# A recurrent attention kernel: its next-memory product moved into column tiles, its first transposes moved from DMA to TensorE, and its order searched again

## Chip, cores, metric

One core of one Trainium2 chip. The metric is device time of one launch in microseconds (us), the median of several executions. A ratio is the mean time of one kernel's runs over the mean of the other's runs of the same rounds, so it isn't quite the ratio of the medians quoted beside it. Where I turn a ratio into microseconds I multiply by 1869, the time before.

## The reference, cut to what matters

```python
def _A_ref(x, mem0, Wq, Wk, Wv, Wo, seg_len):      # S 2048, Dm 512, H 32, Dh 128, M 8, seg 32
    mem = mem0
    for s in range(S // seg_len):                    # 64 segments, one after the other
        h = concatenate([mem, xs])                   # 8 memory rows + 32 tokens
        q, k, v = (einsum('btd,dhe->bhte', h, W) for W in (Wq, Wk, Wv))
        p = softmax(where(mask, q @ k.T * scale, -1e9))
        o = einsum('bhte,hed->btd', p @ v, Wo)
        mem = o[:, :M, :]                            # the memory of the next segment
        outs.append(o[:, M:, :])
# x = x + A(layernorm(x)); x = x + B(layernorm(x)); and both once more
# B: linear attention over all 2048 tokens with 32 heads of 16
```

Layer A is a recurrence: segment s+1 can't be projected before segment s has gone through attention, the output projection and back into `mem`. There are 2 x 64 such steps. B of the first layer must be complete before the second A starts.

## The kernel before

The kernel is a program that writes a program. Every operation is a node with a cost; a list scheduler runs a clock of its own, gives each node an engine and a place, and the places are steered by priorities (`OFFSET`, one number for each node of a step). TensorE's products come in two kinds: the whole 128x128 array ("full"), and column tiles ("col"), where four products of 32 output columns each share the array. The scheduler charges 0.1 us for a change between them.

```python
PE_SWITCH = 0.1
...
            nd.start = max(tn, rtime(nd))
            if e == "pe":
                if nd.mode != self.pe_mode:
                    nd.start += PE_SWITCH
                self.pe_mode = nd.mode
```

A projection is four groups of four products in tiles. Its image is copied out of PSUM and turned, either by a DMA transpose issued from SP or by 16 TensorE transposes and one more copy:

```python
        def turned(W, key, blk, bkeys, b, dst, dkey, urgent, dma):
            tl = project(W, key, blk, bkeys, b, urgent)
            k = img_no[0] % NI if urgent else NI          # the left block has one buffer for all its images
            ...
            nd = evac(img[:, k, :], lambda: tl.f32()[:, :], 512, ...)
            if dma:
                add("sp", lambda e: e.dma_start_transpose(dst..., img[:, k, :]), 1.25, ..., lat=TURN)
                return nd
            ...  # 16 x pe.transpose(..., tile_position=(0, 32 * j)), then evac
```

The four tiles of the output projection each hold a part of the sum over heads (and a half of the columns), so the next memory is the sum over row groups of `outW`, done by a product with a 0/1 matrix. The same `outW` also goes through selection products into the residual (whole array, f32r):

```python
        def next_mem(s, w):
            at(s, "next")
            for h in range(2):
                def mm(pe, h=h):
                    return pe.matmul(tl.f32()[:, 16 * h:16 * h + 16], outW[:, w, 128 * h:128 * h + 128], selm_sb[:, :],
                                     start=True, stop=True)
                add("pe", mm, 0.13, reads=[("outW", w, h), "selm"], tiles=[tl], urgent=True)
            evac(hT[:, G1 % 2, g1, :, 0:8]..., urgent=True)   # into the next segment's input
```

A "left block" collects the last 8 tokens of each of 4 segments, is projected once for 4 steps, and serves as filler for TensorE while the recurrence waits.

The softmax here doesn't subtract the row's maximum and nothing guards it: scores larger than these inputs give would overflow.

## Time and profile before

| | before |
|---|---|
| median, us | 1869.8 (1865.6 to 1870.0, 3 runs) |
| profiled run, span | 1867.5 |
| TensorE / ScalarE / VectorE busy | 94% / 62% / 57% |
| first next-memory product of layer 1 | 60.7 us |
| 62 steps of layer 1 | 831.3 us, 13.41 a step |
| turn to layer 2 (63rd to 64th product) | 67.5 us |
| 62 steps of layer 2 | 841.5 us, 13.57 a step |
| tail | 66.5 us |

The rows of the view by stretches up to the first next-memory product and from there to the last of layer 1 (columns: length, busy time of PE, PEld, DVE, ACT, POOL with counts, granted clock, DMA share, GB/s):

```profile
0.00:60.70 60.70, 29.96 (x478) 14.13 (x478) 12.73 (x35) 16.98 (x44) 13.94 (x61) 0.84 0.93 310
60.70:891.90 831.20, 813.34 (x20871) 562.67 (x20912) 487.35 (x1536) 533.04 (x1393) 25.48 (x47) 1.00 0.21 41
```

Three lines follow. The first is the summary of the page's chain of waits, the shares of the span by engine. The other two are the product that changes, from the view of its source line: weight loads (PEld) and products (PE), count, and the duration in ns as min/median/max.

```profile
PE 85%; DMA 10%; ACT 2%; DVE 2%; issue 1%; SPq 0%; ACTq 0%; DVEq 0%
...
L975 PEld LDWEIGHTS pb<-selm_sb,outW_sb x252: 185/186/337, 60.6 to 1801.3; 128*128 128x128 f32 x126
L975 PE MATMUL pb<-selm_sb,outW_sb x252: 256/277/362, 60.7 to 1801.3; 128*128 128x16 f32 x126
```

There are 252 of them, two for each of 126 steps. A duration is the time from start to modelled end; products overlap, so what one costs the queue is how far it moves the end on, and I use that below ("the advance").

### The profile page before, as it was taken

To read this page: it belongs to the slowest core of one execution; us is meant where nothing else is said; L and a number is where in the kernel's file an instruction comes from. 1 tells how busy PE (TensorE), PEld (TensorE's weight loads), DVE (VectorE), ACT (ScalarE), POOL (GpSimd) and SP (SyncE) were. 2 spreads that over 40 slices of the span, in tenths; PEclk is the share of its full clock that TensorE was granted. 3 is DMA by queue.
4 is the path that set the end of the run, shared out by engine and by line. 5 is a ranking of instruction groups with operands and counts; after the bars stand their busy time and mean duration, and the time that the engine had idled before them with its cause. 6 is when DMAs were issued, how large, how long until landed. Compare 5 with 4: busy or idle time off the path is not lost.

```text
span 1867.5 us, 95161 instructions
## 1 busy us (share of the span) xinstructions
PE 1762.9 (94%) x43796; PEld 1201.8 (64%) x43905; DVE 1065.5 (57%) x3267; ACT 1160.3 (62%) x3015; POOL 74.5 (4%) x172
## 2 busy tenths in 40 slices
PE   4899999999999999999799999999999999999996
PEld 1566767666666667676456666766667666676662
DVE  1455555656565565655445556556555665565555
ACT  2466666666666666666456666666666666666655
POOL 2000000000000000000000000000000000000000
PEclk8999999999999999999899999999999999999999
DMA  9512121221222121211021222122122221212213
GB/s 336 126 35 42 35 43 37 43 40 37 43 37 43 35 46 37 45 38 40 21 42 35 42 38 48 40 37 45 37 44 42 45 43 38 45 38 54 45 34 124
DMA packets 228256, 96.86 MB, mean 52 GB/s; under 512 B 211624, under 2 KB 222000, under 8 KB 226320
## 3 DMA queue, kind: packets, MB, share of 16 engines
q1 hardware_dynamic: 220656, 62.58, 18.1%
q0 software_dynamic: 5616, 15.60, 2.7%
q10 hardware_dynamic: 1584, 12.58, 1.7%
q8 instruction: 343, 5.62, 1.3%
q14 instruction: 57, 0.47, 0.1%
HBM read 29.89 MB, written 10.49 MB: 22 GB/s over the span
## 4 chain that ended last, share of the span: by engine, by line
PE 85%; DMA 10%; ACT 2%; DVE 2%; issue 1%; SPq 0%; ACTq 0%; DVEq 0%
PE pb L753 39%; PE pb L952 15%; DMA arena_sb<-arena_sb 8%; PE pb L928 4%; PE pb L837 3%; PE pb L775 3%; PE pb L993 3%; PE pb L1088 2%; PE pb L975 2%; PE pb L854 2%; PE pb L892 2%; PE pb L1124 1%; PE pb L868 1%; PE pb L1190 1%; PE pb L867 1%
## 5 line engine op out<-in xcount | busy, mean ns | idle before, releaser
L591 ACT ACTIVATE arena_sb<-pb 128x512 bf16<-128x512 f32 (+6 forms) x1309 | 682.0, 530 | 341.5 <-PE pb L753 272.5
L753 PE MATMUL pb<-Wk_sb,arena_sb 128*32 128x512 bf16 x5120 | 347.7, 383 | 5.5 <-DMA Wk_sb<-in_A_Wk_dram 5.5
L753 PE MATMUL pb<-Wv_sb,arena_sb 128*32 128x512 bf16 x5120 | 352.2, 381 | 0.0
L753 PE MATMUL pb<-Wq_sb,arena_sb 128*32 128x512 bf16 x5120 | 342.2, 383 | 5.4 <-DVE arena_sb L592 4.8
L952 PE MATMUL pb<-Wo_sb,arena_sb 128*32 128x256 bf16 x10368 | 312.3, 275 | 4.9 <-DMA Wo_sb<-in_A_Wo_dram 2.9
L592 DVE CAST arena_sb<-pb 128x128 bf16<-128x128 f32 (+3 forms) x452 | 179.9, 398 | 221.3 <-PE pb L975 110.0
L952 PEld LDWEIGHTS pb<-Wo_sb,arena_sb 128*32 128x32 bf16 x10368 | 274.2, 97 | 20.7 <-DMA Wo_sb<-in_A_Wo_dram 3.4
L913 DVE TENSOR_TENSOR arena_sb<-arena_sb 32x256 bf16<-32x256 bf16 x512 | 212.1, 414 | 50.9 <-ACT arena_sb L909 38.8
L592 DVE COPY arena_sb<-pb 128x512 bf16<-128x512 bf16 (+2 forms) x325 | 121.2, 380 | 191.6 <-PE pb L775 183.9
L753 PEld LDWEIGHTS pb<-Wk_sb,arena_sb 128*32 128x32 bf16 x5120 | 136.9, 97 | 133.6 <-DMA Wk_sb<-in_A_Wk_dram 5.6
L753 PEld LDWEIGHTS pb<-Wq_sb,arena_sb 128*32 128x32 bf16 x5120 | 124.2, 96 | 111.3 <-DVE arena_sb L592 10.6
L753 PEld LDWEIGHTS pb<-Wv_sb,arena_sb 128*32 128x32 bf16 x5120 | 132.5, 97 | 98.1 <-issue 2.8
L591 ACT ACTIVATE outW_sb<-pb 128x128 fp32r<-128x128 f32 x228 | 63.2, 277 | 200.0 <-PE pb L952 198.0
L775 PEld LDWEIGHTS pb<-id_sb,arena_sb 128*32 128x32 bf16 x4096 | 76.4, 96 | 95.0 <-ACT arena_sb L591 47.5
L775 PE MATMUL pb<-id_sb,arena_sb 128*32 128x128 bf16 x4096 | 103.1, 220 | 24.1 <-ACT arena_sb L591 20.2
L928 PE MATMUL pb<-arena_sb 128*128 128x128 bf16 x1024 | 118.7, 217 | 5.5 <-DVE arena_sb L915 5.5
L592 DVE CAST outW_sb<-pb 128x128 fp32r<-128x128 f32 x96 | 28.0, 292 | 161.6 <-ACT outW_sb L591 161.6
L915 DVE TENSOR_TENSOR arena_sb<-arena_sb 32x64 bf16<-32x64 bf16 x512 | 110.8, 216 | 15.7
L844 ACT ACTIVATE arena_sb<-pb 128x256 bf16<-128x256 f32 x252 | 92.1, 383 | 41.1 <-PE pb L837 33.1
L929 PE MATMUL pb<-arena_sb 128*128 128x32 bf16 x1024 | 109.7, 178 | 0.0
L928 PEld LDWEIGHTS pb<-arena_sb 128*128 128x128 bf16 x1024 | 87.8, 96 | 7.2 <-DVE arena_sb L915 5.9
L837 PE MATMUL pb<-arena_sb 128*128 128x32 bf16 x2016 | 89.3, 177 | 2.8 <-DMA arena_sb<-arena_sb 2.5
(109 smaller groups left out, 2270.2 us busy)
## 6 DMA issues: line engine op xcount, KB each, us to landing
arena_sb<-arena_sb SPq DMA_TRANSPOSE x384, 2.5
Wq_sb<-in_A_Wq_dram ACTq DMA_DIRECT2D x1, 4096.0 KB, 13.5
Wk_sb<-in_A_Wk_dram ACTq DMA_DIRECT2D x1, 4096.0 KB, 23.7
Wv_sb<-in_A_Wv_dram ACTq DMA_DIRECT2D x1, 4096.0 KB, 34.4
Wo_sb<-in_A_Wo_dram SPq DMA_DIRECT2D x4, 1024.0 KB, 7.5
xs_scratch<-x_sb POOLq DMA_DIRECT2D x32, 128.0 KB, 2.0
pq_scratch<-arena_sb POOLq DMA_DIRECT2D x32, 128.0 KB, 2.5
x_sb<-xs_scratch POOLq DMA_DIRECT2D x16, 128.0 KB, 2.3
```

What stands on the lines that cost most here:

```text
L591: return e.activation(o() if callable(o) else o, i() if callable(i) else i, ACTF.Copy)
L592: return e.tensor_copy(o() if callable(o) else o, i() if callable(i) else i)
L753: r = pe.matmul(tl.f32()[32 * j:32 * j + 32, 0:512], blk[:, c, :], W[:, c, o:o + 512], start=(c == 0), stop=(c == 3), tile_position=(0, 32 ...
L775: r = pe.transpose(tt.bf16()[32 * j:32 * j + 32, 128 * i:128 * i + 128], img[:, k, o:o + 32], id_sb[:, :], tile_position=(0, 32 * j))
L837: r = pe.matmul(tl.f32()[:, o:o + 32], kk[:, hh, :, :].rearrange("p j x -> p (j x)"), qT[:, r2, hh, :, 0:8], start=True, stop=True)
L844: add("act", lambda a: a.activation(Pm[:, k, :, :].rearrange("p a q -> p (a q)"), tl.f32()[:, 0:256], ACTF.Exp, scale=SCALE), c_act(256), ...
L913: add("dve", lambda v, q=q, j=j: v.tensor_tensor(Pbx[q, :, j, 0:32], Px[q, :, :], Rx[q, :, :], ALU.mult), c_dve(256) + 0.075, reads=["Px", ...
L915: add("dve", lambda v, q=q, j=j: v.tensor_tensor(Pbx[q, :, j, 32:40], PLL[q, g2, :, gl], Rx[q, :, 0:8], ALU.mult), c_dve(64) + 0.075, read ...
L928: pe.matmul(o, vimg[:, r2, e], Pbx[:, hh, :, 0:32], start=True, stop=False)
L929: return pe.matmul(o[:, :, 0:8], vleft[:, g2, e], Pbx[:, hh, :, 32:40], start=False, stop=True)
L952: r = pe.matmul(tl.f32()[32 * j:32 * j + 32, 0:256], oT[:, 4 * hh + n, :], Wo_sb[:, 8 * n + hh, 256 * d:256 * d + 256], start=(hh == 0 and ...
L993: r = pe.matmul(tl.f32()[:, 256 * d:256 * d + 256], sel(d), outW[:, u, :], start=first and d == 0, stop=last, skip_group_check=True)
```

## The change

The intent: (1) make the next-memory product cheaper and of the same kind as the products around it, so that the array needn't change between whole and tiles; (2) in the first step and the first left block of each layer transpose on TensorE, since nothing else fills it there; (3) search the priorities again.

```diff
-MODE_SLACK = 13.03
-LOOK = 0.073
+MODE_SLACK = 13.61
+LOOK = 0.082
 ... (every list of OFFSET has new numbers; the first step has lists of its own)
-            P.at(base + s, name + ("F" if s < 0 else "L" if ...))
+            P.at(base + s, name + ("F" if s <= 0 else "L" if ...))
 ...  left_block
-                turned(Wq_sb, "Wq", blk, bk, b, qTl[:, r2, hs, :, :], ("qTl", r2, b), False, True)
+                turned(Wq_sb, "Wq", blk, bk, b, qTl[:, r2, hs, :, :], ("qTl", r2, b), False, step > 0)
 ... (the same for Wk)
 ...  next_mem
                 def mm(pe, h=h):
-                    return pe.matmul(tl.f32()[:, 16 * h:16 * h + 16], outW[:, w, 128 * h:128 * h + 128], selm_sb[:, :],
-                                     start=True, stop=True)
-                add("pe", mm, 0.13, reads=[("outW", w, h), "selm"], tiles=[tl], urgent=True)
+                    for j in range(4):
+                        o = 128 * h + 32 * j
+                        r = pe.matmul(tl.f32()[32 * j:32 * j + 32, 16 * h:16 * h + 16], outW[:, w, o:o + 32].bitcast(F32),
+                                      selm_sb[:, :].bitcast(F32), start=True, stop=True, tile_position=(0, 32 * j))
+                    return r
+                add("pe", mm, 0.075, reads=[("outW", w, h), "selm"], tiles=[tl], urgent=True, mode="col")
 ...  the step
-                turned(Wq_sb, "Wq", blk, bk, b, qT[:, r2, hs, :, :], ("qT", r2, b), True, QDMA[b])
+                turned(Wq_sb, "Wq", blk, bk, b, qT[:, r2, hs, :, :], ("qT", r2, b), True, QDMA[b] and s > 0)
 ... (the same for Wk)
```

## The prediction

> **What bounds the kernel now.** I read the page's busy shares first, then the stretches of its span, then TensorE's groups, and last the two starts in the timeline.
>
> ```profile
> PE 1762.9 (94%) x43796; PEld 1201.8 (64%) x43905; DVE 1065.5 (57%) x3267; ACT 1160.3 (62%) x3015; POOL 74.5 (4%) x172
> ```
>
> TensorE is busy 94% of the span, the next engine 62%. An average hides stages, so I asked for five stretches: until the first output projection, the steps of layer 1 (first to last next-memory product), the turn to layer 2, the steps of layer 2, the tail. The columns are the length, then busy time of each engine, then granted clock.
>
> ```profile
> 0.00:57.20 57.20, 26.46 (x407) 11.36 (x411) 12.73 (x35) 15.83 (x41) 13.94 (x61) 0.85 0.95 317
> 57.20:891.90 834.70, 816.84 (x20942) 565.45 (x20986) 487.35 (x1536) 534.19 (x1396) 25.48 (x47) 1.00 0.21 42
> 891.90:959.50 67.60, 50.53 (x907) 28.61 (x909) 29.27 (x77) 27.95 (x67) 2.92 (x6) 0.85 0.15 31
> 959.50:1801.00 841.50, 824.46 (x20986) 572.07 (x21043) 500.19 (x1546) 549.22 (x1450) 30.95 (x57) 1.00 0.21 42
> 1801.00:1867.50 66.50, 44.56 (x563) 24.32 (x566) 35.96 (x75) 33.09 (x64) 1.22 (x3) 0.92 0.32 96
> ```
>
> In both runs of steps TensorE is busy 98% at full clock: there only work taken from TensorE counts. Both have 62 full steps: 831.3/62 = 13.4 us and 841.5/62 = 13.6 us a step. At the start it is busy 46% of 57 us, and there something else sets the end. The chain of waits on the page gives TensorE 85% and DMA 10%; the DMA part of a step (about 4 us of a transpose) is covered by other TensorE work, so I don't count it as time to win.
>
> **The next-memory product** as one step has it in the timeline (start, length):
>
> ```profile
> 705.96 0.27 PE L892 MATMUL pb<-arena_sb 128*32 128x32 bf16 x16
> 706.16 0.39 PE L975 MATMUL pb<-selm_sb,outW_sb 128*128 128x16 f32 x2
> 706.40 0.48 PE L993 MATMUL pb<-outW_sb,selx_sb 128*128 128x256 f32 x2
> 706.84 0.50 PE L993 MATMUL pb<-outW_sb,sell_sb 128*128 128x256 f32 x2
> 707.19 0.28 PE L904 MATMUL pb<-arena_sb,bo_sb 128*128 128x256 bf16 x1
> 707.31 0.19 PE L905 MATMUL pb<-arena_sb,bo_sb 128*128 128x64 bf16 x1
> 707.43 0.40 PE L753 MATMUL pb<-Wq_sb,arena_sb 128*32 128x512 bf16 x4
> ```
>
> L975 is the product that changes. Lines with 128*32 work in column tiles, those with 128*128 in the whole array; the sequence goes tiles, whole array, tiles.
>
> **The first step of the kernel.** What the SP queue issued, and what TensorE then waited for:
>
> ```profile
> 16.95 2.61 SPq L766 DMA_TRANSPOSE arena_sb<-arena_sb  x2
> 24.96 0.39 SPq L629 DMA_DIRECT2D Wo_sb<-in_A_Wo_dram  x1
> 34.28 7.78 SPq L766 DMA_TRANSPOSE arena_sb<-arena_sb  x3
> 42.11 0.58 SPq L629 DMA_DIRECT2D Wo_sb<-in_A_Wo_dram  x1
> 45.30 1.19 SPq L766 DMA_TRANSPOSE arena_sb<-arena_sb  x1
> 46.53 2.83 SPq L629 DMA_DIRECT2D Wo_sb<-in_A_Wo_dram  x2
> 57.16 0.51 PE L952 MATMUL pb<-Wo_sb,arena_sb 128*32 128x256 bf16 x12 [2.94 <-DMA Wo_sb<-in_A_Wo_dram]
> ```
>
> The first output projection waits for the last quarter of Wo. The quarters landed at 39.6, 49.0, 53.5 and 57.1 us (semaphore events). The second may leave once Wv is there (36.2 us), but stood behind transposes on SP until 42.1.
>
> **What the Trainium skill says.** (1) "TensorEngine Tiling (Array Packing)", Key Properties: changing the tiling mode drains TensorE. The trace agrees: in order of start there are 276 changes each way (2.2 a step). A projection's first four products end 0.22 us after work in tiles and 0.32 after whole-array work; the first L975 ends 0.207 us after tiled work, the second 0.112 after the first. So a change costs about 0.1 us. (2) "FP8 and Floating Point Precision", TensorE Precision Notes: true FP32 takes 4 passes. No plain f32 product is in this trace. (3) "TensorE: Matmul & The Clock Gate", Back-to-back issue gap: starts are never under about 25 ns apart. The trace agrees for whole-array products of 32 columns (25 ns apart); 16 in tiles advance 6.3 ns each, 25 ns for four.
>
> **The change part by part.**
> Next memory: an L975 pair costs 0.112 x 2 = 0.22 us, and its changes 0.1 each way. The selection sums rows, so the new form puts 32 columns of the head-half output into each of four column tiles: 8 products of 16 columns. Four passes for each group of four tiles at the 25 ns floor are 0.10 us, so 0.20 a step; if the passes stream as 64 columns, 0.03 a group and 0.05 a step. Both are estimates; I take 0.15, so the product alone saves 0.07. The larger gain is that the neighbours are also in tiles (output projection before, q projection after), so the pair of changes, 0.2 us, can go, but only where the 0.5 us between this product and the next q is filled with tiled work. With residual and sums (L993, L904) there, as above, the changes stay. Left-block projections are not in every step, so I count three tenths of the steps: 0.06. Together 0.13 x 126 = 16 us, all on the bound engine.
> Start of layer 1: no transposes stand before Wo on SP. The second quarter can leave at 36.2. At the 344 GB/s this queue moved in the stretch when it had only Wo, 1 MB takes 3.05 us: after the first at 39.6, the others land at 42.7, 45.7, 48.8. V, due 36.2, and the 26 us of TensorE work before L952 fit, since TensorE had 31 us idle there. 57.1 - 48.8 = 8 us off the path.
> Start of layer 2: from 930.7 to 959.5 step 0 takes 28.8 us against a later 13.4, with TensorE busy 24.8 of it at clock 0.86. The left block's four transposes share one image buffer and each holds it for some 4 us (median landing 2.5 us after issue). On TensorE a set of 16 takes 0.23 us of throughput and a copy of 0.42. At most 4.0 idle and 24.8 x 0.14 = 3.5 us of low clock can be won; 6 x 0.23 = 1.4 us is added. I take 3 net.
> Order: work at its own pace (each product at the median spacing of its kind) sums to 1617 us, the changes to 552 x 0.1 = 55; ends and turn leave about 105 idle. Some 90 us, 0.7 a step, remain as small stalls. The search of before could not remove them; I give the new one 4.
> Sum: 16 + 8 + 3 + 4 = 31, so 1869.8 - 31 = 1839 us.
>
> **The rivals.** (a) *The changes stay and f32 is slow.* If a pass is dearer than the floor, the product saves nothing, and if full-array fill sits before and after it, two more changes come: 0.2 x 126 = 25 us lost. For it: steps without left work have only L904, L905 and L993 to fill. Against: the order is chosen to avoid it. Only starts would gain: 1855 to 1865. (b) *Wo doesn't bound the first step.* If V at half clock (1.9 us for 16 products at 41 us) bounds it, the first step gains 4 instead of 8: 1843. (c) *Every pair of changes goes.* Then 0.27 x 126 = 34 us and the starts: 1820. Against it: the residual must run in the whole array somewhere, though it could join the memory attention. (d) *A transpose by DMA becomes the wait.* When TensorE takes less time a step, its 4 us cover may fail. TensorE's slack of 2% says the cover is good now; a loss would be some tenths a step, giving 1850.
>
> **Range and chances.** The product is worth 5 to 30 us, the first start 4 to 10, the second 0 to 6, the order -5 to 12; they're independent, so roughly +-18 on the sum: 1821 to 1857. Over 2% faster means below 1832.4, a third of a range's width below my centre: 0.28. Slower than 1907 needs a broken order: 0.01.
>
> **What would show it.** L975 in tiles: the time from the end of the work before it to its last product under 0.2 us against 0.32; mode changes below 2.2 a step, toward 1.8; the first output projection near 49 us; first L975 of layer 2 some 3 us sooner after the layer's start; a step of 13.2 to 13.3 us against 13.4 and 13.6; no other engine over 70%. I am wrong if f32 products in tiles have long starts (over 0.1 us a group), if Wo still lands after 53 us, or if the step gains over 0.25 us.

## The result, and the profile after

The changed kernel takes 1854.2 us (median of 4, 1851.7 to 1855.9) against 1869.3 (4 runs): ratio 0.9922, 95% interval 0.9905 to 0.994. That is 14.6 us less, where I had forecast 31. The span of the profiled run is 1850.0 us.

The view by stretches of the changed kernel, cut at the same events as in the table above (length, busy time of PE, PEld, DVE, ACT, POOL, then granted clock, DMA share, GB/s):

```profile
0.00:54.60 54.60, 31.69 (x604) 16.65 (x604) 15.35 (x43) 18.09 (x47) 13.97 (x61) 0.91 0.90 324
54.60:883.60 829.00, 810.60 (x21712) 551.82 (x21752) 469.05 (x1478) 557.76 (x1447) 25.22 (x46) 1.00 0.21 42
883.60:941.70 58.10, 45.92 (x970) 27.23 (x973) 28.16 (x75) 26.31 (x65) 3.26 (x6) 0.88 0.08 20
941.70:1783.70 842.00, 826.36 (x21904) 561.11 (x21962) 492.15 (x1492) 571.96 (x1514) 30.64 (x56) 1.00 0.22 42
1783.70:1850.00 66.30, 45.72 (x578) 24.44 (x580) 36.66 (x76) 33.17 (x64) 1.62 (x3) 0.89 0.32 94
```

| stretch | before | after | difference | forecast |
|---|---|---|---|---|
| to the first next-memory product | 60.7 | 54.6 | -6.1 | -8 |
| 62 steps, layer 1 | 831.3 | 829.0 | -2.3 | -20 for both layers: product 16, order 4 |
| turn | 67.5 | 58.1 | -9.4 | -3 |
| 62 steps, layer 2 | 841.5 | 842.0 | +0.5 | |
| tail | 66.5 | 66.3 | -0.2 | 0 |

So nearly the whole gain sits at the start and the turn, and 124 of the 128 steps gained 1.8 us together. (These differences sum to 17.5 us; the profiled run was the fastest of its four.)

The product itself, from the view of its source line:

```profile
L988 PEld LDWEIGHTS pb<-selm_sb,outW_sb x2016: 106/108/113, 54.6 to 1783.8; 128*32 128x32 f32 x184
L988 PE MATMUL pb<-selm_sb,outW_sb x2016: 177/182/204, 54.6 to 1783.9; 128*32 128x16 f32 x184
```

Eight plain f32 products a step leave 16 records, two for each. Their advance is 0.14 us a step in layer 1 and 0.12 in layer 2, where the old pair had 0.34 and 0.33. But the old figure held the change of tiling in front of it, 0.9 a step at 0.1 us; the pair itself was 2 x 0.112 = 0.22. So the product alone saves about 0.10 us a step, a little over the 0.07 that I had put down, and whether the change is saved as well is seen only from all changes together. And one step of the timeline, to set beside the one in the prediction:

```profile
692.18 3.79 PE L963 MATMUL pb<-Wo_sb,arena_sb 128*32 128x256 bf16 x128
695.79 0.28 PE L988 MATMUL pb<-selm_sb,outW_sb 128*32 128x16 f32 x16
696.01 0.28 PE L915 MATMUL pb<-arena_sb,bo_sb 128*128 128x256 bf16 x1
696.13 0.19 PE L916 MATMUL pb<-arena_sb,bo_sb 128*128 128x64 bf16 x1
696.16 0.49 PE L1007 MATMUL pb<-outW_sb,selx_sb 128*128 128x256 f32 x2
696.57 1.05 PE L764 MATMUL pb<-Wq_sb,arena_sb 128*32 128x512 bf16 x16
```

L988 now follows the output projection without a change. But the sums (L915, L916) and the residual (L1007) still stand between it and the q projection (L764), in the whole array, so there is a change into them and one out of them, as before. In the program's order 122 of 126 steps have whole-array work between L988 and L764, and from the output projection to the next q projection a step has 2.14 changes, where every step had exactly 2 before. The rest of the step, with the turn between the layers counted in, went from 2.26 to 2.83. Together, counted over the matmul records in order of start, the changes went from 276 to 324 each way: from 4.15 and 4.08 a step (both directions, layers 1 and 2) to 4.85 and 4.74. I had expected fewer.

The start of layer 1, SP's issues and the first output projection:

```profile
25.75 11.32 SPq L640 DMA_DIRECT2D Wo_sb<-in_A_Wo_dram  x2
37.16 1.30 SPq L777 DMA_TRANSPOSE arena_sb<-arena_sb  x1
38.56 4.29 SPq L640 DMA_DIRECT2D Wo_sb<-in_A_Wo_dram  x2
...
50.75 3.47 PE L963 MATMUL pb<-Wo_sb,arena_sb 128*32 128x256 bf16 x64 [2.83 <-issue]
```

Wo's second quarter left as soon as Wv was there (both at 36.7 us), and the quarters landed at 38.6, 42.5, 47.4 and 50.7 us (before: 39.6, 49.0, 53.5, 57.1). The first output projection began at 50.75 us, right behind the last landing, where it had begun at 57.16. The line's "issue" hides that landing. The granted clock was 0.54 over these 64 products, and they took 3.47 us, where 1.93 is usual at full clock. In the kernel before, the same 64 took 2.90 us at 0.64, so only 0.57 us of this is new.

The start of layer 2, before and after: from the transpose of the layer norm to the next-memory product.

```profile
930.76 0.61 PE L728 MATMUL pb<-id_sb,arena_sb 128*128 128x128 bf16 x4 [2.74 <-DVE arena_sb L722]
...
958.01 1.06 PE L952 MATMUL pb<-Wo_sb,arena_sb 128*32 128x256 bf16 x32 [0.34 <-DVE arena_sb L871]
...
959.45 0.60 PE L975 MATMUL pb<-selm_sb,outW_sb 128*128 128x16 f32 x2
```

```profile
921.22 0.61 PE L739 MATMUL pb<-id_sb,arena_sb 128*128 128x128 bf16 x4 [2.74 <-DVE arena_sb L733]
...
939.98 1.06 PE L963 MATMUL pb<-Wo_sb,arena_sb 128*32 128x256 bf16 x32
...
941.65 0.32 PE L988 MATMUL pb<-selm_sb,outW_sb 128*32 128x16 f32 x16
```

28.7 us became 20.4. TensorE's busy time in it fell from 24.8 to 20.3 us and its idle time from 3.9 to 0.2; 192 projection products stand in it, where 240 did. Without the DMA transposes, which waited for each other in one image buffer, the second half of the output projection came 18.8 us after the layer norm in place of 27.3.

### The profile page after: what moved, and what is told of

It is laid out like the page before. It is cut to its first block, busy times and chain, and to the rows that moved or that the text cites. A ratio compares the mean times of both kernels' runs of the same rounds, so it can differ in the third digit from the quotient of the medians.

```text
span 1850.0 us, 99018 instructions
## 1 busy us (share of the span) xinstructions
PE 1760.3 (95%) x45752; PEld 1181.3 (64%) x45861; DVE 1041.4 (56%) x3161; ACT 1207.3 (65%) x3133; POOL 74.7 (4%) x172
## 4 chain that ended last, share of the span: by engine, by line
PE 84%; DMA 11%; ACT 2%; DVE 2%; issue 1%; ACTq 0%; SPq 0%; DVEq 0%
PE pb L764 38%; PE pb L963 16%; DMA arena_sb<-arena_sb 9%; PE pb L939 4%; PE pb L848 4%; PE pb L786 3%; PE pb L1007 3%; PE pb L865 2%; PE pb L1102 2%; PE pb L903 2%; ACT arena_sb L602 2%; PE pb L1138 1%; PE pb L879 1%; DMA Wk_sb<-in_A_Wk_dram 1%; PE pb L878 1%
## 5 line engine op out<-in xcount | busy, mean ns | idle before, releaser
L602 ACT ACTIVATE arena_sb<-pb 128x512 bf16<-128x512 f32 (+6 forms) x1369 | 704.7, 525 | 337.9 <-PE pb L764 269.7
L764 PE MATMUL pb<-Wk_sb,arena_sb 128*32 128x512 bf16 x5120 | 345.4, 381 | 4.8 <-DMA Wk_sb<-in_A_Wk_dram 4.6
L764 PE MATMUL pb<-Wq_sb,arena_sb 128*32 128x512 bf16 x5120 | 342.9, 383 | 4.7 <-DMA Wq_sb<-in_A_Wq_dram 0.6
L764 PE MATMUL pb<-Wv_sb,arena_sb 128*32 128x512 bf16 x5120 | 345.1, 379 | 0.3 <-issue 0.3
L963 PE MATMUL pb<-Wo_sb,arena_sb 128*32 128x256 bf16 x10368 | 324.2, 275 | 5.4 <-issue 3.0
L603 DVE CAST arena_sb<-pb 128x128 bf16<-128x128 f32 (+3 forms) x411 | 161.9, 394 | 246.0 <-PE pb L988 152.3
L963 PEld LDWEIGHTS pb<-Wo_sb,arena_sb 128*32 128x32 bf16 x10368 | 266.5, 97 | 28.2 <-DVE arena_sb L882 13.4
L764 PEld LDWEIGHTS pb<-Wk_sb,arena_sb 128*32 128x32 bf16 x5120 | 132.3, 97 | 128.4 <-DMA Wk_sb<-in_A_Wk_dram 4.8
L764 PEld LDWEIGHTS pb<-Wq_sb,arena_sb 128*32 128x32 bf16 x5120 | 120.8, 97 | 116.2 <-DVE arena_sb L1131 6.1
L602 ACT ACTIVATE outW_sb<-pb 128x128 fp32r<-128x128 f32 x287 | 79.8, 278 | 170.3 <-PE pb L963 139.1
L764 PEld LDWEIGHTS pb<-Wv_sb,arena_sb 128*32 128x32 bf16 x5120 | 130.9, 97 | 88.3 <-issue 1.6
L855 ACT ACTIVATE arena_sb<-pb 128x256 bf16<-128x256 f32 x252 | 96.5, 384 | 43.7 <-PE pb L848 35.2
L786 PE MATMUL pb<-id_sb,arena_sb 128*32 128x128 bf16 x4288 | 107.2, 221 | 16.6 <-ACT arena_sb L602 12.5
L882 DVE TENSOR_TENSOR arena_sb<-pb,arena_sb 128x128 bf16<-128x128 f32 x252 | 72.7, 289 | 43.2 <-ACT arena_sb L870 24.2
L848 PEld LDWEIGHTS pb<-arena_sb 128*128 128x128 bf16 x2016 | 72.4, 96 | 27.9 <-DMA arena_sb<-arena_sb 9.4
```

Of the source, the lines that this page charges most:

```text
L602: return e.activation(o() if callable(o) else o, i() if callable(i) else i, ACTF.Copy)
L603: return e.tensor_copy(o() if callable(o) else o, i() if callable(i) else i)
L764: r = pe.matmul(tl.f32()[32 * j:32 * j + 32, 0:512], blk[:, c, :], W[:, c, o:o + 512], start=(c == 0), stop=(c == 3), tile_position=(0, 32 ...
L786: r = pe.transpose(tt.bf16()[32 * j:32 * j + 32, 128 * i:128 * i + 128], img[:, k, o:o + 32], id_sb[:, :], tile_position=(0, 32 * j))
L848: r = pe.matmul(tl.f32()[:, o:o + 32], kk[:, hh, :, :].rearrange("p j x -> p (j x)"), qT[:, r2, hh, :, 0:8], start=True, stop=True)
L855: add("act", lambda a: a.activation(Pm[:, k, :, :].rearrange("p a q -> p (a q)"), tl.f32()[:, 0:256], ACTF.Exp, scale=SCALE), c_act(256), ...
```

## The experiments

Twelve kernels ran, all within the reference's tolerance (those with wrong values too). "Frozen" means that the scheduler is told the old costs and kinds and only the emitted instructions differ, so every instruction stands where it stood. The intervals of the ratios are about 0.2% either way, 3.5 us.

My theory after the traces had two parts. The changes of tiling rose and took back much of what the product saved. And a step isn't set by TensorE alone: its queue and the recurrence's latency (copies out of PSUM, transposes, softmax) are balanced against each other, so time cut from TensorE comes back in part as waiting. The rivals: the new order is at fault and the product would have paid its full 0.2 x 126 = 25 us in the old one; or the starts gained by the order and not by the transposes. When I wrote these expectations I still took all of the 0.2 us for the product's own saving; half of it is the change in front of it, so the sums in them that start from 0.2 are high by that.

**The product alone, in the old order (`b_prod`).** The next-memory product of the change in the kernel before, cost and kind as they were told before, frozen.

> The kernel before with the new next-memory product alone, every instruction of every engine in the place it had (the scheduler is still told the old cost and kind, so the order is frozen). The product's own time should fall from 0.33 us a step to about 0.13. My theory: the places it stands in have whole-array work beside them, so changes of tiling rise from 4.1 to about 5.0 a step (0.09 us), the rest comes back as waits on the recurrence, and the two runs of 62 steps lose no more than 4 us together; total 1864 to 1870. Rival (the new order is to blame, the product itself is worth its TensorE time): 0.2 x 126 = 25 us, or 14 us after the added changes: 1844 to 1856.

Measured: 1875.1 us, ratio 1.0036 (1.0019 to 1.0054): 6.7 us slower. The stretches of the two runs of steps:

```profile
60.90:897.80 836.90, 818.41 (x21786) 562.59 (x21785) 487.89 (x1537) 534.01 (x1393) 25.61 (x47) 1.00 0.21 41
...
964.40:1808.60 844.20, 831.53 (x21913) 574.06 (x21913) 500.25 (x1546) 549.81 (x1450) 31.00 (x57) 1.00 0.21 42
```

Layer 1 takes 5.6 us and layer 2 2.7 us more. Product, residual and first sum together had 0.91 us of advance a step in layer 1 before and 0.89 now: what the product saved, the changes at its neighbours took (4.84 and 5.13 a step in all). The trace shows where: in 59 of these 124 steps whole-array products, often the sums (L904, L905), stand between the two halves, and a half in tiles then needs a change into tiles and one out again. The new pair's own advance is 0.22 us here, where it is 0.12 to 0.14 in the changed kernel. From the end of the last output projection product to the start of the next q projection a step takes 1.64 us on average in the kernel before, 1.64 here, and 1.43 in the changed kernel. So the rival falls: in the old order the product is worth nothing. Why it is even slower than my estimate of no gain, I can't say.

**The old product in the new order (`a_oldprod`).** Frozen.

> The changed kernel with the old product put back (two whole-array f32r products), order frozen. The product costs 0.2 us a step more and stands between tiled work, so changes rise from 4.8 to about 6.5 a step (0.17 us). Both theories expect it slower; if all 0.37 us a step showed, 126 steps would give +47 us (1901). My theory, in which part of TensorE's time a step is slack: +25 to +35 us, 1880 to 1890. If the product didn't matter at all: under +10 us.

Measured: 1892.7 us, ratio 1.0137, so 40 us over the changed kernel, more than my theory's 25 to 35 and less than the full 47. Changes are 6.56 and 6.48 a step. In the new order a whole-array product stands among tiles, so going back costs 0.10 us for the product and 1.7 changes, which makes 34 to 36 us of the 40 (an estimate, at the 0.10 to 0.11 us a change that `a_switch` gives below). The new order needs the new product, though product and order together gained the steps next to nothing.

**The starts without TensorE's transposes (`a_dmastart`), and these transposes alone in the kernel before (`b_start`).** Here the order can't be frozen, since instructions come and go.

```diff
 a_dmastart, in the changed kernel
-  ("qTl", r2, b), False, step > 0)              # and kTl
+  ("qTl", r2, b), False, True)
-  ("qT", r2, b), True, QDMA[b] and s > 0)       # and kT
+  ("qT", r2, b), True, QDMA[b])
 b_start: the reverse, in the kernel before; the new entries take the priority of the DMA they replace
```

> The changed kernel with the first step and the first left block of each layer transposed by DMA again, the order chosen anew by the same priorities. My theory: the first next-memory product goes from 54.6 us back toward 60 us, and the turn between the layers from 58 us back toward 64 to 67 us; total +8 to +15 us, 1862 to 1869. Rival (the gain at both starts came from the new order and not from the transposes): under +4 us.

> The kernel before with only the first step and the first left block of each layer transposed on TensorE; old product, old priorities (the new entries take those of the DMA they replace). My theory: first next-memory product 4 to 7 us earlier, the turn 5 to 9 us shorter, steps unchanged or up to 4 us worse in layer 2 since its order was not searched: 1853 to 1862. Rival (only the new order gained): 1866 to 1872.

| us | before | b_start | after | a_dmastart |
|---|---|---|---|---|
| first next-memory product | 60.7 | 57.1 | 54.6 | 64.5 |
| turn | 67.5 | 60.2 | 58.1 | 64.8 |
| 62 steps, layer 1 | 831.3 | 837.8 | 829.0 | 833.9 |
| 62 steps, layer 2 | 841.5 | 851.1 | 842.0 | 844.4 |
| ratio to before | 1 | 1.0021 | 0.9922 | 1.0030 |

Each time the start and the turn move with the transposes: 3.6 and 7.3 us in the old kernel, 9.9 and 6.7 in the new. That rival falls too. But both totals missed my expectations: `a_dmastart` lost 20 us in place of 8 to 15, as its steps also took 7 us more, and `b_start` is 4 us slower than the kernel before in place of 7 to 16 faster, as its steps took 16 us more. By its total alone `b_start` would have confirmed the rival; only the stretches speak against it. Its order wasn't searched, which is the likely reason for the slower steps, though no run separates that from the other effects of a new order. So what the search seems worth here is that the steps stay where they were.

**A little work cut from TensorE (`b_trim`, `a_trim`).** The last of the four groups of each left-block projection at 32 columns in place of 512, frozen: 192 x 0.19 = 36.5 us of filler in tiles less, no change of tiling touched.

```diff
-  r = pe.matmul(tl.f32()[32 * j:32 * j + 32, 0:512], blk[:, c, :], W[:, c, o:o + 512],
-                start=(c == 0), stop=(c == 3), tile_position=(0, 32 * j))
+  n = 32 if c == 3 and not urgent else 512
+  r = pe.matmul(tl.f32()[32 * j:32 * j + 32, 0:n], blk[:, c, :], W[:, c, o:o + n],
+                start=(c == 0 or n == 32), stop=(c == 3 or (c == 2 and not urgent)), tile_position=(0, 32 * j))
```

> The kernel before, order frozen, with the last quarter of each left-block projection cut from 512 to 32 columns (wrong results on purpose): 192 groups of four products, 0.216 - 0.026 = 0.19 us of TensorE each, 36 us in all, in tiles, without any change of tiling added or removed. If TensorE's throughput sets the step: -33 to -36 us against before. My theory (part of TensorE's time is filler under the recurrence): about half of it, -15 to -22 us.

> The changed kernel, order frozen, with the same cut (wrong results on purpose; 36 us of TensorE work less). Throughput: -33 to -36 us against the changed kernel. My theory, that the recurrence carries more of the step than before: clearly less than in the kernel before, -8 to -15 us, and the step of layer 1 stays above 13.2 us.

Measured: `b_trim` 0.9912 (16 us less), `a_trim` 0.9860, so 12 us less than the changed kernel at 0.9922. The runs of steps of `b_trim`, then of `a_trim`:

```profile
61.80:885.60 823.80, 802.32 (x20871) 557.53 (x20912) 488.75 (x1536) 533.86 (x1393) 25.62 (x47) 1.00 0.21 41
...
950.50:1782.90 832.40, 811.68 (x20985) 565.14 (x21042) 500.79 (x1547) 550.00 (x1450) 30.93 (x57) 1.00 0.22 42
```

```profile
55.40:879.70 824.30, 803.60 (x21714) 546.03 (x21752) 469.54 (x1478) 556.84 (x1447) 25.15 (x46) 1.00 0.22 42
...
935.00:1773.40 838.40, 818.47 (x21904) 554.20 (x21962) 492.45 (x1492) 569.71 (x1514) 30.55 (x56) 1.00 0.23 43
```

The 36.5 us are an estimate from the advances in the trace. Taken from an engine that is busy 98%, they bring 16 us in the kernel before (45%) and 12 in the changed one (32%). Within the steps alone it is 7.5 + 9.1 = 16.6 us before and 4.7 + 3.6 = 8.3 after. The cut didn't arrive whole, though. From the start of each cut group to the start of the next product the traces show 32.7 us less before and 27.5 after; in 56 of the 192 places of `a_trim` the next-memory product follows, and starts 156 ns after the start of the cut group, where a projection in that place starts after 28 ns. Of what left the queue 50% and 42% came back, and 16 and 12 us are within each other's intervals: that the two kernels differ here isn't shown.

**A little work added (`b_more`, `a_more`).** One group of each left-block projection computed a second time, frozen: 192 x 0.216 = 41.5 us.

```diff
+  if c == 3 and not urgent:
+      for j in range(4):      # the same four products again, start=True, stop=True
```

> The kernel before, order frozen, with one quarter of each left-block projection computed a second time (wrong results on purpose): 192 groups of 0.216 us added, 41 us of TensorE work. Throughput: +39 to +43 us. If there were slack in TensorE: clearly less, under +25. My theory: nearly all of it, +35 to +40, since work added anywhere in a queue that is in order delays what stands behind it; only cuts run into the recurrence.

> The changed kernel, order frozen, with the same addition (wrong results on purpose, 41 us of TensorE work more). Throughput: +39 to +43 us against the changed kernel; my theory: +35 to +40, as in the kernel before.

Measured: 1.0204 (38 us more) and 1.0157 (44 us over the changed kernel). Work added counts at 92% and 106% (the 44 us is a little above the 35 to 40 that I expected). So the kink is where the kernel stands: adding costs all of it, cutting brings about half.

**More changes of tiling (`a_switch`).** One whole-array product of 8 columns behind the first half of the next memory, frozen; results stay right.

```diff
+  if h == 0:
+      r = pe.matmul(tl.f32()[:, 64:72], one_sb[:, :], one_sb[:, 0:8], start=True, stop=True)
```

> The changed kernel, order frozen, with one whole-array product of 8 columns put behind the first half of each next-memory product, where tiled work stands on both sides (its output is not read; results stay right). 126 products of at most 0.06 us, 3 to 7 us in all, and 248 more changes of tiling (from 648 to 896). If a change costs 0.1 us as the transitions in the trace say and work added counts in full, as in the two runs with added work: +28 to +32 us against the changed kernel, so 1882 to 1886. If changes cost nothing: +3 to +7 us.

Measured: 1887.1 us, ratio 1.0087: 31 us over the changed kernel. Less 3 to 7 us for the 126 products, 248 changes cost 24 to 28 us, 0.10 to 0.11 each. The 0.7 changes a step that the change brought are thus worth 0.07 to 0.08 us a step, 9 us in 124 steps.

**Less latency, the same work (`a_halfcopy`, `b_halfcopy`).** The copies of the urgent q and k images out of PSUM at half width after the first six, frozen: wrong values, no TensorE instruction differs.

```diff
+  n = 256 if urgent and img_no[0] > 6 else 512
-  nd = evac(img[:, k, :], lambda: tl.f32()[:, :], 512, ...)
+  nd = evac(img[:, k, 0:n], lambda: tl.f32()[:, 0:n], 512, ...)
```

> The changed kernel, order frozen, with every urgent copy of a q or k image out of PSUM at half width after the first six (wrong results on purpose): about 0.2 us less latency for four copies a step, no TensorE work, no change of tiling touched; ScalarE is busy 65% and doesn't bound. If TensorE's throughput alone sets the step: within 2 us of the changed kernel. My theory, that waits inside the recurrence carry part of the step: 4 to 12 us less, 1842 to 1850.

> The kernel before, order frozen, with the same half-width image copies as the run on the changed kernel (wrong results on purpose), which saved that one 16.5 us without touching TensorE's work. If the new order took the product's saving back by leaning more on the recurrence than the old one did, the old order gains less here: -4 to -12 us, 1857 to 1865. If both lean on it alike: -14 to -19 us.

Measured: `a_halfcopy` 1837.7 us, ratio 0.9818, 19 us less than the changed kernel; `b_halfcopy` 1854.2 us, ratio 0.9922, 15 us less than the kernel before. The runs of steps of `a_halfcopy`:

```profile
55.90:877.70 821.80, 812.47 (x21754) 556.86 (x21750) 461.24 (x1478) 511.40 (x1447) 25.14 (x46) 1.00 0.22 42
...
935.80:1771.80 836.00, 828.45 (x21964) 565.40 (x21962) 480.99 (x1492) 527.83 (x1515) 30.55 (x56) 1.00 0.23 43
```

With the same work on TensorE and a ScalarE that is busy two thirds of the time, the steps became shorter by 7.2 and 6.0 us. TensorE's busy time didn't fall; what fell is the rest, from 18.4 to 9.3 us in layer 1. (The rows show 13 us of the 19: the profiled run of the changed kernel was the fastest of its four, that of `a_halfcopy` the slowest.) So something other than TensorE's work sets part of the step, which a kernel bound by TensorE's throughput alone would not show. I take it for latency inside the recurrence; but a shorter copy also frees ScalarE (46 us less in layer 1) and the copy's PSUM tile sooner, and no run separates these. The 19 us are also more than the 4 to 12 that I expected. The steps of `b_halfcopy` are shorter by 6.5 and 6.4 us. My finer expectation, that the new order leans on it clearly more than the old one, isn't shown: 19 and 15 us are within the intervals of each other.

**A further search (`a_search`).** The changed kernel with the product's cost told as 0.055 a half and some 3000 tries more on the priorities.

> The changed kernel with the product's cost in the scheduler lowered from 0.075 to 0.055 us a half (the trace shows 0.11 to 0.14 a step with its waits) and the order searched a little further, about 3000 tries; changes of tiling stay at 4.8 a step. My theory, that the order is already near a balance of TensorE and recurrence that none of these small moves breaks: 0 to 6 us less than the changed kernel, ratio to the kernel before 0.989 to 0.992. If the step had a large slack that a cheaper product opens: 10 us or more, ratio under 0.987.

Measured: 1849.7 us (6 runs), ratio 0.9902 (0.9882 to 0.9922). It is the lowest of the right kernels, but its interval touches that of the changed kernel, so I don't call it faster than that.

## Why the prediction was wrong, point by point

**The changes of tiling: the step that failed.** I wrote "the pair of changes, 0.2 us, can go", and "I count three tenths of the steps: 0.06". One step of 126 has no change left between output projection and q. The residual and the sums kept their whole-array stretch in the others, and the new order has more changes than the old one: 0.1 a step more there and 0.6 in the rest of the step. Why the search settled for those isn't shown. That makes 0.7 a step more, and at the 0.10 to 0.11 us that `a_switch` measured some 0.07 us a step, 9 us in all, the wrong way. My forecast for the term was -0.06 us a step, the runs show +0.07.

**The product.** 0.07 forecast, about 0.10 measured: 12 us in 124 steps. This term was near. Together with the changes it leaves 0.03 us a step of TensorE, 4 us, where I had 0.13 and 16 us. The trace shows 1.8 us, and the difference of 2 us is inside the scatter of single runs (the four of the changed kernel span 4.2 us).

**The bound.** "There only work taken from TensorE counts" was too simple, a second fault that the first one hid. I read it off 98% busy at full clock. The runs show that TensorE's time counts in full when it grows (92% and 106%), at about half (50% before, 42% after) when filler is cut, and that shorter copies count with no TensorE work changed. Had my 16 us come off TensorE, 7 to 8 us would have shown (an estimate from the two trims). It is open whether that rate holds for the product: the trims cut filler, and the next-memory product is a link of the recurrence itself. The busy share can't tell: a product's record is 0.1 to 0.3 us longer than what it costs the queue (0.28 against 0.11 for L975, 0.38 against 0.05 for a product of a projection), so a wait of that length between two products stays inside busy time. In `a_trim` some 13 us of layer 1's work were cut (an estimate: its share of the 27.5), and its busy time fell by 7.

**The order.** Forecast 4 us in the steps; the two runs of steps together gained 1.8 us from everything. The trial without a search (`b_start`, 16 us lost in the steps) suggests that the search was needed to keep the steps where they were. It could not make them shorter, and some 3000 more tries brought nothing clear of noise.

**Layer 1's start.** The mechanism was right: Wo no longer stood behind transposes and bounded the first step. Forecast landing 48.8 us, measured 50.7; 6.1 us gained against 8. The 344 GB/s behind my 3.05 us a quarter was misread: the view has it for the first 14.3 us, in which Wq and x came in, and not for a stretch with Wo alone. After the first quarter they took 3.9, 5.0 and 3.2 us; that is the missing 1.9 us.

**Layer 2's start.** Undersized: 9.4 us against 3. My ceiling was 7.5 us of idle time and low clock in the 28.8 us of step 0, and that step alone lost 8.3. I had counted idle TensorE where the chain of transposes through one buffer was the end. The projections that filled its waiting, 48 products of 240, don't stand in the step any more: as many projection products as before precede the step, and 48 more follow it.

**The sum.** The starts gave 15.5 us where I had 11, and the steps 1.8 where I had 20. That the total isn't further off is luck: the second start's excess covers part of what the steps lacked. (A slip in the chances: 1832.4 lies 6.6 us below my centre, a fifth of the range's width and not a third.)

**The rivals.** (a), that the changes stay, came true and more came, though the f32 product isn't slow; "Against: the order is chosen to avoid it" is where I turned it down. (b), that Wo doesn't bound the first step, fell: the first output projection again began right behind Wo's last landing. (c), that every pair goes, didn't happen. (d), a DMA transpose that becomes the wait, isn't shown as such; `a_halfcopy` shows only that something beside TensorE's work counts.

## What to carry to other kernels

Here a share of busy time near 100% said that added work would show; it didn't say that removed work would. Before counting on a cut, cut some harmless work in a frozen order and see what rate comes back, check in the trace that the cut itself arrived, and do the same for a latency; in a schedule that a search has balanced, a cut may not be worth its full size, as here. A cheaper kind of product is worth what its neighbours let it be: count the changes of array mode in the order that will really run.

## What the Trainium skill lacked or had wrong

- "FP8 and Floating Point Precision", TensorE Precision Notes, gives 4 passes for true FP32. Here each plain f32 product in a column tile left two load and product records (2016 of each for 1008 products), and the 16 of a step advance TensorE by 0.12 to 0.14 us. Whether two passes hide in each record, no run shows. The page has no times for small products of this kind.
- "TensorEngine Tiling (Array Packing)", Key Properties, says that a change of tiling mode drains the array, without a size. Here it costs 0.10 to 0.11 us (248 more changes and 126 small products: 31 us), as the transitions in the trace say.
- "TensorE: Matmul & The Clock Gate" gives a weight load's time as its columns over 1.2, from which I estimate 107 ns for 128 and 27 ns for 32. The records are 186 ns for 128 columns of f32r and 96 of bf16, and 97 (bf16) and 108 ns (f32) for 32 columns in a tile, though four tiles advance together.
- "Perfetto Trace Analysis", Identifying the Most-Contended Engine, warns that TensorE's busy share is no good measure of how close it is to its limit, which I had passed over; no page says what a cut at a busy share of 98% brings. Here 27 to 33 us less in the queue brought 12 to 16 us, and 41.5 us more work cost 38 to 44.
